# Score copies moved ahead of exponentials in five steps of a batch, and loads of rows and v placed in other steps

## The chip, the core and the metric

The kernel runs on one core of a Trainium2 chip. The core has five engines that run side by side, each with its own queue of instructions: TensorE (PE: matmuls, with its weight loads shown as PEld), VectorE (DVE), ScalarE (ACT), GpSimd (POOL) and SyncE (SP, which only issues transfers here). Matmul results land in a small memory called PSUM and have to be copied out of it by DVE or ACT. Transfers between DRAM and the on-chip memory are DMAs; they are issued by SP, ACT or POOL.

The metric is device time in microseconds, the median over runs of the whole kernel. Three runs of the kernel before took 2294.4, 2296.27 and 2301.48 us.

## The reference

Attention over 8 batches, 12 heads, 448 positions and 64 elements a head, with two small matrices that mix the heads, before and after the softmax; then a Fourier mixing over positions and channels with a two-layer network behind it.

```python
scores = scale * np.matmul(q, k.transpose(0, 1, 3, 2))
scores = np.einsum('bhij,hg->bgij', scores, w_pre)
attn = np.exp(scores - np.max(scores, axis=-1, keepdims=True))
attn = attn / (np.sum(attn, axis=-1, keepdims=True) + 1e-09)
attn = np.einsum('bhij,hg->bgij', attn, w_post)
x = np.matmul(attn, v)          # to (B, S, H * D)
...
u = x + np.real(np.fft.fft(np.fft.fft(x, axis=1), axis=2))
un = (u - mean(u)) / np.sqrt(var(u) + 1e-06)
out = u + np.maximum(un @ w_ch1, 0.0) @ w_ch2
```

All data is float32.

## The kernel before

The kernel has two phases. `mix_phase` does attention and the Fourier mixing and takes the first third of the time; `ffn_phase` does the network, with products of half and quarter blocks combined by sums (a Strassen scheme), so that its results are added up from several partial tiles.

**Attention in steps.** A batch is cut into 8 blocks of rows, and these into 23 steps (`GS`); 8 batches make 184 steps (`TOT`), numbered on through all batches. A main loop goes through the steps and emits the instructions of PE, DVE, ACT and POOL in an order that is kept as written (`manual_schedule`); each engine works its own queue in that order. In each step there are, for different positions of a pipeline:

- `pre` (L656): matmuls that mix the heads of the step two ahead, into two PSUM tiles `mx` of one buffer each. `max0` and `max1` (L663, DVE) take the row maxima, `exp0` and `exp1` (L670, ACT) the exponentials with their sums. A `mx` tile is free for the next step's `pre` when its exponential is done.
- `scale` (L677, L678 on DVE, L680 on POOL): the reciprocal of the sums, which needs both exponentials, and the scaling of the two halves.
- `post` (L690) and `turn` (L703, DVE): the second mixing of heads and its turning.
- `QK` (L628): the score matmuls of a block that comes eight steps later. Each call writes two of the four PSUM slots named `ms`, and leaves two copies from PSUM to `Sb` on ACT (L489). The copies are not emitted at once: they go into a list, `pend`.
- `AV` (L720), in 12 of 23 steps, and `full`: transposes of q and k (L601) and of results (L764), and the Fourier matmuls (L829, L845). All of them use `ms` slots, too.
- `gather` (L645): four DMAs on SP that bring the rows of one step out of `Sb` into `Kr`, five steps ahead. A block's `Sb` buffer is used again two blocks later; its first copy then waits for the last gather of the block before.
- `conv` (L250 to L310): one operation on DVE of a conversion of the network's weights.

`flush()` emits what stands in `pend`. It is called after `post`, before each `full` item, before a gather that needs a copy still pending, and at the end of odd steps. The orders of even and odd steps (by the global number, so that a batch step changes its parity from batch to batch) are:

```python
ORDERS = tuple(o.split() for o in (
    "pre post flush AV max0 exp0 "
    "QK max1 exp1 turn scale conv full gather",
    "pre post flush max0 max1 QK exp0 "
    "AV turn exp1 scale conv gather full flush"))
```

**Loads.** `due("none", at, fn)` puts a load at the beginning of step `at`. POOL issues most of them: rows of q and k of the next batch (`emit_load_qk`, two DMAs of 112 KB a call, two calls a tile, into four buffers `raw`), v (`emit_load_v`, one DMA of 224 KB a call), and in the last batch the first rows of the second phase (`lead.load`, into the same four buffers; their statistics are taken from step 5 of that batch on). For batch 0, q, k and v are loaded at step -40, ahead of everything; for batch 1 the first two row tiles follow at step -12. The six tiles of a batch's rows are transposed at steps 5, 9, 13, 15, 15 and 16 of the batch before.

**The end.** In `second2` the last tile's partial results are put on a timetable of numbered places (`on(place, ...)`), one for each matmul and some between. The very last tile has three output quarters, `v11`, `v12` and `v22`, that collect partial sums `j0` to `j6` on DVE (`vec`) or POOL (`pl`) with `both` (L1366) and `more` (L1357), and are stored by SP and ACT, one half each (`store`, L1373).

Of the kernel before, what the change touches and what calls it, by code (L numbers as in the profile page):

```python
# [45 lines left out]
GS = BLOCK_AT[-1]  # L46
# [42 lines left out]
AT_T = ((5, 9), (15, 16), (13, 15))  # L89
AT_L = ((-8, -7), (-6, -5), (-4, -3), (-2, -1), (8, 9), (10, 11))  # L90
AT_V = ((2, 3), (4, 4), (5, 6))
AT_L1 = ((-12, -12), (-12, -12), (2, 3), (4, 5), (8, 9), (10, 11))
AT_QK0 = {2: (-1, 0, 0), 3: (2, 3, 3), 4: (4, 5, 5)}
AT_QK = ((0, 2, 1), (0, 1, 2), (0, 1, 2), (1, 2, 2),
         (0, 1, 2), (0, 1, 2), (0, 1, 2), (0, 1, 2))
AT_AV = ((1, 2, 4), (0, 1, 3), (1, 3, 5), (1, 3, 4))
AT_X = ((13, 0), (23, 1), (28, 3), (29, 2))
AT_Z = (39, 40, 40, 42)
AT_S = ((42, 44), (46, 48))
# [351 lines left out]
def mix_phase(ctx, tc, rest, ident, q, k, v, w_pre, w_post, u_scr, u_rev, wts, lead):  # L451
# [39 lines left out]
    def flush():  # L491
        while pend:
            pend.pop(0)[1]()

    def room(n):
        if sum(e[0] for e in pend) + n > 4:
            flush()
# [79 lines left out]
    def emit_load_v(b, pr, y):  # L577
        if y == 0:
            batches[b]["v", pr] = pvv.tile([P, 2, C7 * D], F32, name="vv", tag=f"vv{pr}")
        h = 6 * y + 2 * pr  # L580
        nc.gpsimd.dma_start(
            out=batches[b]["v", pr][64 * y:64 * y + 64, :, :],
            in_=v[b, h:h + 2].rearrange("h (p c) d -> p h (c d)", c=C7))
# [301 lines left out]
    def due(kind, at, fn):  # L885
        fill[kind].append((at, len(fill[kind]), fn))
# [4 lines left out]
    for b in range(B):  # L891
        f = b * GS
        at_t = [(a, nm, xx) for xx, at in enumerate(AT_T) for nm, a in zip("qk", at)]
        if b == 0:

            for i, xx in enumerate(START):
                for j, nm in enumerate("kq"):
                    for y in range(2):
                        due("none", -40, lambda xx=xx, nm=nm, y=y: emit_load_qk(0, xx, nm, y))
                    due("full", 2 * i + j - 20, lambda xx=xx, nm=nm: emit_xpose(0, xx, nm))  # L900
                for n, at in enumerate((2 * i - 18, i - 13)):
                    due("QK", at, lambda n=n, xx=xx: (emit_qk(n, xx), n))
            for pr in range(3):
                for y in range(2):
                    due("none", -40, lambda pr=pr, y=y: emit_load_v(0, pr, y))
        else:
            for at, (a, nm, xx) in zip(AT_L if b > 1 else AT_L1, sorted(at_t, key=lambda e: e[0])):
                for y in range(2):
                    due("none", f + at[y] - GS if b > 1 else at[y],
                        lambda b=b, xx=xx, nm=nm, y=y: emit_load_qk(b, xx, nm, y))  # L910
            for xx, at in enumerate(AT_T):
                for nm, a in zip("qk", at):
                    due("full", f + a - GS,
                        lambda b=b, xx=xx, nm=nm: emit_xpose(b, xx, nm))
        for pr in range(3 if b else 0):
            for y in range(2):
                due("none", f + AT_V[pr][y], lambda b=b, pr=pr, y=y: emit_load_v(b, pr, y))
        for n in range(0 if b else 2, NBL):
            for xx in range(3):
                due("QK", AT_QK0[n][xx] if b == 0 and n in AT_QK0 else  # L920
                    f + BLOCK_AT[n] - 8 + AT_QK[n][xx],
                    lambda n=NBL * b + n, xx=xx: (emit_qk(n, xx), n))
        for n in range(NG):
            for pr in range(3):
                due("AV", f + GROUP_AT[n + 1] + AT_AV[n][pr],
                    lambda a=b * NG + n, pr=pr: (emit_av(a, pr), None))
            at, gi = AT_X[n]
            if b == B - 1 and n > 1:
                at += 2
            due("full", f + at, lambda g=groups[b * NG + gi]: emit_x(g))  # L930
        for n, at in enumerate(AT_Z):
            due("full", f + at, lambda b=b, n=n: emit_z(b, n // 2, n % 2))
        for pair in range(2):
            for par in range(2):
                due("full", f + AT_S[pair][par],
                    lambda b=b, pair=pair, par=par: emit_s2(b, pair, par))
    f = (B - 1) * GS
    due("none", f + 1, lambda: nc.gpsimd.memset(lead.mhalf[:, :], -0.5))
    for x in range(TB // P):
        for y in range(2):  # L940
            due("none", f - 4 + 2 * x + y, lambda x=x, y=y: lead.load(x, y))
        due("full", f + (5, 9, 11, 13)[x], lambda x=x: [lambda: lead.stats(x)])
        due("full", f + (15, 16, 19, 21)[x], lambda x=x: [lambda: lead.norm(x)])
        due("full", f + 18 + 2 * x, lambda x=x: lead.turn(x, ms_tile))
# [11 lines left out]
    def take(kind, s):  # L956
        large = 0
        while fill[kind] and fill[kind][0][0] <= s:
            fn = fill[kind].pop(0)[2]
            if kind == "none":  # L960
                large += bool(fn())
            elif kind == "full":
                flush()
                pend.extend((1, e, None) for e in fn())
            else:
                room(2)
                evs, n = fn()
                pend.extend((1, e, n) for e in evs)
        return large

    s = int(min(v_[0][0] for v_ in fill.values()))
    ET = mybir.EngineType
    with tc.manual_schedule(engines={ET.PE, ET.DVE, ET.Activation, ET.Pool}):
        while s <= TOT - GS + AT_X[-1][0]:
            old = len(later)
            n = take("none", s)
            ahead, now = 0 <= s + LM < TOT, 0 <= s < TOT
            for op in ORDERS[s % 2]:
                if op == "flush":
                    flush()  # L980
                elif op in fill:
                    take(op, s)
                elif op == "conv":
                    if s >= 4:
                        wts.deal(1)
                elif op == "gather":
                    if 0 <= s + LG < TOT:
                        if any(e[2] is not None and e[2] <= at_step[s + LG][0] for e in pend):
                            flush()
                        emit_gather(s + LG)  # L990
                elif op == "scale":
                    if ahead:
                        emit_scale(s + LM)
                    for _ in range(old if s < TOT + 5 else 0):
                        later.pop(0)()

                    if s < TOT - 3:
                        for _ in range(min(len(folds), 1 if n and s > 3 else 2)):
                            folds.pop(0)()
                elif op in ("post", "turn"):  # L1000
                    if now:
                        (emit_postmix if op == "post" else emit_turn)(s)
                elif ahead:
                    (emit_premix if op == "pre" else emit_max if op[0] == "m"
                     else emit_exp)(s + LM, *map(int, op[3:]))
            s += 1
        flush()
        wts.deal(1000)
# [42 lines left out]
def ffn_phase(ctx, tc, rest, ident, u_scr, u_rev, wts, ub_scr, out, fold_rest,  # L1051
# [262 lines left out]
    def second2(n, st):  # L1314
# [5 lines left out]
        vec = nc.vector  # L1320

        def on(s, fn, *a):
            at.setdefault(s, []).append(lambda: fn(*a))
# [52 lines left out]
        for j, i in enumerate(ORDER2):  # L1376
            b = 7 * j
# [13 lines left out]
        j0, j3, j5, j6, j4, j1, j2 = range(7)  # L1391
        v22, v12, v11 = range(7, 10)
        pl = nc.gpsimd
# [5 lines left out]
        if end:  # L1399
            for v, r, d in ((v11, 0, 0), (v12, 0, 1), (v22, 1, 1)):  # L1400
                on(0, load, v, r, d)
            on(27, out_, j3, 1, 0)
            on(41, both, vec, j6, j5)
            on(41, out_, j6, 1, 0)
            for s, *o in ((24, vec, v11, j0), (33, vec, j5, j0), (34, pl, v12, j5),
                          (41, pl, v22, j6), (44, vec, v12, j4), (51.5, vec, v11, j1),
                          (59, vec, v22, j4)):
                on(s, both, *o)
            on(52, store, v11, 0, 0)
            on(58, store, v12, 0, 1)  # L1410
            on(60, store, v22, 1, 1)
        else:
            for s, *o in ((33, j5, j0), (40, j6, j5), (47, j5, j4), (54, j0, j1),
                          (61, j5, j2), (62, j4, j6)):
                on(s, both, vec, *o)
            on(27, out_, j3, 1, 0)
            on(44, out_, j6, 1, 0)
            on(55, out_, j0, 0, 0)
            on(62, out_, j5, 0, 1)
            on(63, out_, j4, 1, 1)  # L1420
# [133 lines left out]
```

## Time and profile before

| What | us |
|---|---|
| median of three runs | 2296.27 |
| the profiled execution | 2299.42 |
| its span, first to last instruction | 2297.6 |
| PE busy | 2249.2 |
| DVE busy | 1711.2 |
| POOL busy | 1292.1 |
| ACT busy | 1167.1 |
| PE on the chain that ended last | 87% of the span |

The profile belongs to one execution. Its lines are read as follows. A line of the timeline has the start in us from the beginning of the span, the duration, the engine, the line of the kernel, the operation, the tiles it writes and reads (`out<-in`), their shapes, a count, and in brackets the idle time of the engine before it with what ended that. A line of the waits has who waited, for whom, the total in us, how often, and the longest. SP's and ACT's issuing of DMAs is marked SPq and ACTq.

Batches 1 to 6 of attention take 94 to 97.5 us each between their first premix matmuls, batch 0 takes 87.2; a step is 2.5 to 6.1 us long, most are 3.3 to 4.7.

### The profile page before, as it was taken

The numbers are of one execution on the slowest core, as the hardware profiler recorded it, in microseconds if no ns is written. First come the engines' busy times: TensorE is split into PE (matmuls) and PEld (weight loads), VectorE is DVE, ScalarE is ACT, GpSimd is POOL, SyncE is SP. The second block draws the span as 40 slices with busy tenths as digits, with TensorE's granted clock in tenths as the row PEclk, the third lists the DMA queues.
The fourth block names the chain that finished last, engine by engine and source line by source line (L and its number), as shares of the span: only waits on it lengthen the run. The fifth ranks groups of instructions, "written<-read, shape, count | busy, mean of one in ns | idle before, by whom it ended". The sixth has DMA issues, their size and how long they took to land.

```text
span 2297.6 us, 60793 instructions
## 1 busy us (share of the span) xinstructions
PE 2249.2 (98%) x22894; PEld 1740.7 (76%) x22894; DVE 1711.2 (74%) x3640; ACT 1167.1 (51%) x3330; POOL 1292.1 (56%) x1805
## 2 busy tenths in 40 slices
PE   7999999999999999999999999999999999999998
PEld 3455555555554677777899999999999899999998
DVE  5778787888877757776877787778778777765545
ACT  4676767767676533231445445444444445434434
POOL 7677878879768541221555555546555645454334
PEclk9999999999999999999999999999999999999999
DMA  7566565666756475649677887788787987795664
GB/s 185 168 178 181 168 192 171 190 179 181 202 151 190 143 265 182 230 162 327 191 181 180 252 214 184 212 195 242 204 197 184 277 188 174 191 257 121 143 146 76
DMA packets 228063, 439.45 MB, mean 191 GB/s; under 512 B 35964, under 2 KB 149558, under 8 KB 227772
## 3 DMA queue, kind: packets, MB, share of 16 engines
q1 hardware_dynamic: 156620, 301.52, 38.2%
q0 software_dynamic: 68864, 133.00, 30.4%
q8 instruction: 183, 3.00, 0.6%
q10 hardware_dynamic: 2288, 1.05, 0.2%
q14 instruction: 108, 0.88, 0.1%
HBM read 213.16 MB, written 143.16 MB: 155 GB/s over the span
## 4 chain that ended last, share of the span: by engine, by line
PE 87%; DVE 5%; DMA 3%; ACT 2%; issue 1%; POOL 1%; SPq 1%; ACTq 0%; DVEq 0%; POOLq 0%
PE psP L1213 18%; PE psP L1335 14%; PE psR L1213 9%; PE psR L1335 7%; PE mx L656 6%; PE ms L720 6%; PE ms L628 5%; PE po L690 5%; PE psQ L1213 4%; PE psQ L1335 3%; PE psP L1290 3%; PE ms L845 2%; PE ms L601 2%; DMA Kr<-Sb 1%; PE psR L1290 1%
## 5 line engine op out<-in xcount | busy, mean ns | idle before, releaser
L1369 POOL DMA_DIRECT2D out_dram<-od x172 | 209.1, 1276 | 261.7 <-DVE od L1357 175.3
L680 POOL TENSOR_SCALAR PP<-PP,rcp 128x448 f32<-128x448 f32 x368 | 234.6, 647 | 170.2 <-DVE rcp L678 123.8
L670 ACT ACTIVATE PP<-mx,nmx 128x448 f32<-128x448 f32 x368 | 230.2, 631 | 165.2 <-DVE nmx L663 157.2
L663 DVE TENSOR_REDUCE nmx<-mx 128x1 f32<-128x448 f32 x368 | 212.5, 618 | 101.2 <-PE mx L656 99.1
L1176 POOL TENSOR_TENSOR hq<-h 128x128 f32<-128x128 f32 (+1 forms) x210 | 130.0, 619 | 255.9 <-ACT h L1235 122.3
L1363 ACT COPY od<-psP 128x192 f32<-128x192 f32 x488 | 156.1, 320 | 172.0 <-PE psP L1335 170.6
L1366 DVE TENSOR_TENSOR od<-od 128x768 f32<-128x768 f32 x210 | 201.3, 972 | 52.7 <-ACT od L1363 52.3
L703 DVE STREAM_TRANSPOSE Pv<-po 128x896 f32<-128x896 f32 x184 | 203.7, 1107 | 2.9 <-PE po L690 2.1
L489 ACT COPY Sb<-ms 124x448 f32<-124x448 f32 (+1 forms) x378 | 181.7, 540 | 46.0 <-PE ms L628 19.2
L656 PE MATMUL mx<-Kr,kw 60*32 60x448 f32 x2944 | 192.2, 549 | 4.3 <-ACT PP L670 2.3
L628 PE MATMUL ms<-kT,qT 64*32 64x448 f32 (+1 forms) x3072 | 191.6, 545 | 3.9 <-ACT qT L489 2.8
L720 PEld LDWEIGHTS ms<-Pv,vv 64*64 64x64 f32 x5376 | 138.1, 132 | 73.7 <-issue 48.8
L690 PE MATMUL po<-PP,kw 60*32 60x448 f32 x2944 | 184.0, 537 | 1.2 <-POOL PP L680 1.1
L1213 PE MATMUL psP<-qs,w1t 128*128 128x256 f32 x744 | 179.2, 380 | 2.4 <-DVE h L1234 1.5
L1213 PE MATMUL psP<-ks,w1t 128*128 128x256 f32 x744 | 179.3, 380 | 0.4 <-DVE h L1234 0.3
L720 PE MATMUL ms<-Pv,vv 64*64 64x120 f32 (+1 forms) x5376 | 160.8, 263 | 3.6 <-ACT Sb L489 2.2
L254 POOL TENSOR_SCALAR wst<-wst 128x256 f32<-128x256 f32 (+1 forms) x76 | 118.6, 1569 | 67.2 <-ACT wst L265 66.9
L1213 PEld LDWEIGHTS psP<-qs,w1t 128*128 128x128 f32 x744 | 139.5, 190 | 19.4 <-DVE h L1234 1.9
L1213 PEld LDWEIGHTS psP<-ks,w1t 128*128 128x128 f32 x744 | 139.5, 190 | 17.2 <-DVE h L1234 0.7
L1213 PE MATMUL psP<-ub,w1t 128*128 128x256 f32 x528 | 127.2, 379 | 1.1 <-DVE h L1234 1.1
L1234 DVE TENSOR_TENSOR h<-h,psP 128x512 f32<-128x512 f32 x42 | 28.8, 686 | 127.9 <-PE psP L1213 112.3
L1335 PE MATMUL psP<-w2t,hq 128*128 128x192 f32 x490 | 122.5, 332 | 1.2 <-DVE od L1357 1.2
(199 smaller groups left out, 5301.6 us busy)
## 6 DMA issues: line engine op xcount, KB each, us to landing
Kr<-Sb SPq DMA_DIRECT2D x730, 105.0 KB
out_dram<-od POOLq DMA_DIRECT2D x172, 384.0 KB, 6.3
qs<-ub SPq DMA_DIRECT2D x89, 384.0 KB
ks<-ub SPq DMA_DIRECT2D x88, 384.0 KB
ub<-ub SPq DMA_DIRECT2D x79, 384.0 KB
w1t<-w SPq DMA_DIRECT2D x42, 384.0 KB
w2t<-w SPq DMA_DIRECT2D x42, 384.0 KB
raw<-in_moe_w_ch_dram SPq DMA_DIRECT2D x32, 384.0 KB
```

Source lines behind the costliest of these rows:

```text
L628: nc.tensor.matmul(pss[x][o:o + hi - lo, :S], st["qT", xx][64 * x:64 * x + 64, y, lo:hi], st["kT", xx][64 * x:64 * x + 64, y, :], start=Tr ...
L656: nc.tensor.matmul(mx[x][64 * z + o:64 * z + o + 32, :S], kw1[64 * x:64 * x + KR, o:o + 32], Kr[64 * x:64 * x + KR, z, :], start=True, sto ...
L663: nc.vector.tensor_reduce(nmx[:, :], steps[T]["mx"][x][:, :S], axis=AX.X, op=ALU.max, negate=True)
L670: nc.scalar.activation(steps[T]["PP"][:, x, :], steps[T]["mx"][x][:, :S], ACTF.Exp, bias=steps[T]["nmx", x][:, :], accum_out=steps[T]["den ...
L680: nc.gpsimd.tensor_scalar(PP[:, x, :], PP[:, x, :], rcp[:, x:x + 1], 1.0, op0=ALU.mult, op1=ALU.mult)
L690: nc.tensor.matmul(po[o:o + 32, z, :S], kw2[64 * z:64 * z + KR, y, :], PP[64 * z:64 * z + KR, :, c * HS:(c + 1) * HS], start=True, stop=True)
L703: nc.vector.transpose(turned[a]["Pv"][:, j, :].rearrange("p (z s) -> p z s", z=2), steps[T]["po"][:, :, :S])
L720: nc.tensor.matmul(pss[y][64 * x:64 * x + 64, :nu * R], st["v", pr][64 * y:64 * y + 64, x, jb * D:(jb + 1) * D], _ap(Pv, 64 * y * rp + 32 ...
L1213: mm = nc.tensor.matmul(p[:, m, :], w1[i][:, kc, m * P:(m + 1) * P], ub[:, kc, :], start=i in (0, 4, 1)[:3 - seed] and m == kc == 0, stop= ...
L1335: nc.tensor.matmul(ps[j, key][:, :DQ], a, b, start=m in (0, 4), stop=True, skip_group_check=True)
L1366: eng.tensor_tensor(D[j][:, :, :], D[j][:, :, :], D[k][:, :, :], op=ALU.add)
L1369: nc.gpsimd.dma_start(out=acc[t, r, d], in_=D[j][:, :, :], accum_op=ALU.add)
```

## The change

It makes four edits.

- A new list `TWO` names steps 0, 2, 5, 13 and 15 of a batch. In these, from step 0 on, `flush()` is called right after `QK`. In odd steps this places the copies of the scores on ACT before both exponentials, in even steps between the first and the second. Without it they come behind both.
- Batch 0's v is loaded at steps 0, 1, 3 and 4 instead of -40 (`AT_V0`), and all six row tiles of batch 1 get other steps (`AT_L1`): the first at -2 and -1, the others from 2 to 12.
- The first rows of the second phase are loaded four steps earlier, from step -8 relative to the last batch.
- In the last tile, the sum of `j6` into `v22` goes from POOL (place 41) to DVE (43), that of `j4` into `v22` from DVE (59, the last sum of all) to POOL (45), and `v22` is stored at place 57, ahead of `v12` at 58.

```diff
-AT_L1 = ((-12, -12), (-12, -12), (2, 3), (4, 5), (8, 9), (10, 11))
+AT_L1 = ((-2, -1), (2, 4), (5, 6), (7, 8), (9, 10), (11, 12))
+AT_V0 = ((0, 0), (1, 1), (3, 4))
...
+TWO = (0, 2, 5, 13, 15)
...
-            for pr in range(3):
-                for y in range(2):
-                    due("none", -40, lambda pr=pr, y=y: emit_load_v(0, pr, y))
...
-        for pr in range(3 if b else 0):
+        for pr in range(3):
             for y in range(2):
-                due("none", f + AT_V[pr][y], lambda b=b, pr=pr, y=y: emit_load_v(b, pr, y))
+                due("none", f + (AT_V if b else AT_V0)[pr][y], lambda b=b, pr=pr, y=y: emit_load_v(b, pr, y))
...
-            due("none", f - 4 + 2 * x + y, lambda x=x, y=y: lead.load(x, y))
+            due("none", f - 8 + 2 * x + y, lambda x=x, y=y: lead.load(x, y))
...
                 elif op in fill:
                     take(op, s)
+                    if op == "QK" and s >= 0 and s % GS in TWO:
+                        flush()
...
             for s, *o in ((24, vec, v11, j0), (33, vec, j5, j0), (34, pl, v12, j5),
-                          (41, pl, v22, j6), (44, vec, v12, j4), (51.5, vec, v11, j1),
-                          (59, vec, v22, j4)):
+                          (43, vec, v22, j6), (44, vec, v12, j4), (45, pl, v22, j4),
+                          (51.5, vec, v11, j1)):
                 on(s, both, *o)
             on(52, store, v11, 0, 0)
             on(58, store, v12, 0, 1)
-            on(60, store, v22, 1, 1)
+            on(57, store, v22, 1, 1)
```

## The prediction

> **What bounds the kernel now.** I read the page first: TensorE (PE) is busy 98% of the span and holds 87% of the chain that ended last, so only what makes PE wait, or what runs after its last matmul, can change the time.
>
> ```profile
> span 2297.6 us, 60793 instructions
> PE 2249.2 (98%) x22894; PEld 1740.7 (76%) x22894; DVE 1711.2 (74%) x3640; ACT 1167.1 (51%) x3330; POOL 1292.1 (56%) x1805
> ```
>
> The change lies in the attention part (to about 830 us) and in the last 12 us. So next the busy time by stretches of that part (columns: stretch, its length, then busy us and count of PE, PEld, DVE, ACT, POOL, the clock, the DMA share, GB/s), and PE's waits from 126 to 770 us (total, times, longest).
>
> ```profile
> 345.00:460.00 115.00, 113.01 (x2390) 61.41 (x2392) 91.92 (x200) 81.56 (x257) 94.55 (x150) 1.00 0.60 181
> ```
>
> ```profile
> PE ms L601 <- ACT Sb L489: 6.5, 17, 1.2
> PE ms L845 <- ACT Sb L489: 2.7, 6, 0.6
> PE ms L720 <- ACT Sb L489: 1.5, 1, 1.5
> PE po L690 <- POOL PP L680: 1.1, 4, 0.4
> ```
>
> The reader sees that PE runs almost gapless, that VectorE (DVE) is 80% busy beside it, and that the waits the copies' move aims at (a transpose or a second-FFT matmul waiting for a PSUM slot that holds scores) sum to 6.5 + 2.7 = 9.2 us, 0.4% of the span. Going through them by step, they sit in batch steps 2, 5, 13 and 15, all in the new list; step 0, also in it, shows none but a 1.1 us "issue" wait.
>
> Then one such step in the timeline, batch 4's step 5 and the step after (DVE, then ACT):
>
> ```profile
> 434.28 1.16 DVE L663 TENSOR_REDUCE nmx<-mx 128x1 f32<-128x448 f32 x2 [0.97 <-PE mx L656]
> 435.36 1.11 DVE L703 STREAM_TRANSPOSE Pv<-po 128x896 f32<-128x896 f32 x1
> 436.45 0.16 DVE L677 TENSOR_REDUCE rcp<-den 128x2 f32<-128x4 f32 x1
> 436.64 0.17 DVE L678 RECIPROCAL rcp<-rcp 128x2 f32<-128x2 f32 x1
> 436.72 1.29 DVE L310 TENSOR_TENSOR wst<-wst 128x256 f32<-128x256 f32 x1
> 437.94 1.12 DVE L489 COPY qT<-ms 128x512 f32<-128x512 f32 x1
> 438.89 1.11 DVE L663 TENSOR_REDUCE nmx<-mx 128x1 f32<-128x448 f32 x2
> ```
>
> ```profile
> 435.00 0.63 ACT L670 ACTIVATE PP<-mx,nmx 128x448 f32<-128x448 f32 x1 [0.46 <-DVE nmx L663]
> 435.63 0.62 ACT L670 ACTIVATE PP<-mx,nmx 128x448 f32<-128x448 f32 x1
> 436.24 0.96 ACT L489 COPY Sb<-ms 124x448 f32<-124x448 f32 x2
> ```
>
> DVE has no idle mark between 435.36 and the next step's max at 438.89: it goes on without a gap behind the reciprocal, and the reciprocal needs both exponentials.
>
> Last, ACT's wait in batch 7 and the tail:
>
> ```profile
> 729.68 0.97 ACT L489 COPY Sb<-ms 124x448 f32<-124x448 f32 x2 [3.66 <-DMA Kr<-Sb]
> ...
> 2291.72 1.73 SPq L1373 DMA_DIRECT2D out_dram<-od  x3
> ...
> 2292.14 0.95 DVE L1366 TENSOR_TENSOR od<-od 128x768 f32<-128x768 f32 x1
> ```
>
> **What the Trainium skill says.** "Perfetto Trace Analysis", section "Matmuls": independent matmul groups should rotate through PSUM banks so that one's evacuation overlaps the next one's matmuls. The trace agrees: the waits above occur just where the rotation over four `ms` slots comes back to a slot not yet copied. "DVE: scalar operands, raw-bit mode, write accounting and state across instructions", section 5: the DVE's queue is one in-order queue. So a late reciprocal holds all behind it; the seven DVE lines above run in program order. "DMA: Bandwidth & Descriptors", section "Issuing engines are not separate DMA queues": transfers from every issuing engine run on the same 16 engines and interleave. The trace agrees: with GpSimd's (POOL's) loads in flight, four of its six first gathers take 2.8, 3.7, 4.0 and 4.0 us to land.
>
> **Part 1, the copies in front.** In a listed step two (in doubled steps four) score copies of 0.41 us spacing go before both exponentials (odd global steps) or before the second (even ones). Worked for batch 4's step 5, an odd one, from t = 433.28 (first premix matmul). Scores start at 434.79; a copy can start 1.07 later (432.51 to 433.58 one step earlier): 435.86, second copy 436.27, exponentials 436.69 and 437.31, the last done with its accumulator read at 438.03. Gain: the transpose starts at 436.50, not 436.82 (0.32). Price: the reciprocal runs at 438.05, not 436.45 (+1.6), and behind it queue the weight operation (1.22 to the next start), the qT copy (0.95) and the next max, now 440.5. Its exponential ends at 441.9; the premix after next needs that PSUM slot and started at 440.99 before. So PE loses 0.9 to 1.1. With a short weight operation (0.27) the same sum ends at about even.
>
> The other listed steps, same method. Odd step 13: gain 0.3, next step longer (3.85, with AV), so the lateness is hidden: -0.1. Odd step 15: two DVE copies queue behind, and the next scores need the slot of the first: +0.5. Even steps 5, 13, 15: the reciprocal is only 1.0 late, -0.3 each where the weight operation is short. Step 2: 0.3 to 0.4 gained, given back through four 0.47 us DVE sums before the next max: +0.1 even, +0.4 odd. Step 0: no wait to gain; 0 even, +0.3 odd. Over batches 2, 4, 6 about +1.0 each; over 1, 3, 5 about 0; batch 7 +0.7: +3.7. All gains without prices: -9.2; prices at the long weight operations throughout: +7.5.
>
> Batch 0 has no slack yet on ACT: four copies at 39.70 to 41.53 follow the exponentials. In front of the second one (done 39.5), they push it to 41.4 and the reciprocal with it; the next exponential starts 1.1 later; step 2 repeats this with two copies (+1.0). The scores of step 3 and the gather at 49.77, which wait for them, come 2.1 later. SyncE then issues gathers back to back to 70, so nothing wins it back: +2.1 (0 if the gathers were not the limit). Steps 13 and 15 there: +0.4.
>
> **Part 2, the loads.** Taken from POOL's queue before 24 us: six v loads of 224 KB, eight row loads of 112 KB (all six row tiles of batch 1 get new steps). From 4 to 24 us the DMA share is above 1.0; the first premix waits to 28.08, 29.63 and 30.01 for gathers. At 2.6 us a gather (the shortest landing among the lead rows' loads) the last, issued at 26.58, is there at 29.2 instead of 30.0: -0.7 (bounds 0 and -1.2). They come back in steps -2 to 12. POOL's issues (0.6 and 0.72 each) lie beside its waits of 2 to 3 us for the reciprocal. Their 2.2 MB compete with gathers, one of which PE awaits for 1.0 us until 59.92: I take +0.3 (-0.5 to +1.5). The lead rows go four steps ahead, from about 682..715 to 665..698. The 16 DMA engines' share is 0.40 from 660 to 700 and 0.80 from 700 to 732, so they leave the full stretch for an empty one. The copy at 729.68 waits for a gather whose issue ended at 722.48, 7.1 us earlier, while POOL moved v, rows and weights; batch steps 6 and 7 there last 0.5 and 2.65 longer than in other batches. But batch 7 also lacks a transpose in step 5 (3.26 against 4.45), so its gathers have less time anyway: of 3.1 us I take -2.2 (0 to -3.1). The moved loads' buffers are free by then (transposes two steps ahead).
>
> **Part 3, the tail.** The 0.95 us sum at 2292.14 leaves DVE's end; one of 0.96 enters at 2286.4. Of it 0.67 fills a wait for ACT, the rest delays by 0.25 all that follows. SyncE issues three stores, the last at 2293.12. After: the first at 2291.97, v22's behind it 0.53 later, v12's next at 2293.0: -0.1 (bounds -0.6 and +0.5). POOL's sum takes the place of its former one (2288.35 to 2290.62) and is hidden.
>
> **Sum.** -0.7 + 0.3 - 2.2 + 2.1 + 0.4 + 3.7 - 0.1 = +3.5 us, against the profiled execution's 2299.42 (span 2297.6, 1.8 around it). That execution is 3.2 above the median 2296.27; on the median: 2299.8, stated as 2299.5.
>
> **The rivals.** Forecast, no change, 0.42: prices and gains cancel. A measurement of this kernel can tell about 0.3% (7 us) from no change, so from 2289.4 to 2303.2.
> Rival A, faster, 0.34: DVE's lateness is absorbed (it is idle 20%, and a weight operation shrinks when it slides off POOL's work), so all 9.2 us of slot waits go, with part of the half-hidden stretch before each (up to 3 more), and batch 7's 3.1 and the start's 0.7: -14, about 2283; the middle of this case is 2285. For it: max starts on PE's release in most steps. Against: the gapless DVE lines in step 5.
> Rival B, slower, 0.24: the reciprocal behind delayed exponentials becomes the bound. Place: DVE between reciprocal and next max in steps 0, 2, 5 and 15; price +7.5, with batch 0's +2.5 and crowded gathers +1.5, nothing won in batch 7: +11, about 2307. It decides once the wait of next max exceeds 1 us in a step followed by a short one.
> That the change doesn't do what it says: the copies could already be forced out by a gather; in listed steps the gather needs an older block, so no.
>
> Eight in ten: 2283 to 2309, from both rivals' ends; the forecast's own range is 2291 to 2303. Faster 0.34, same 0.42, slower 0.24.
>
> **What would show it.** Right: PE waits of L601 and L845 on ACT Sb nearly gone; the DVE reciprocal waiting 1.0 to 1.6 us for ACT PP in listed steps, odd ones more; premix waits on ACT PP growing by several us; the gather of step 3 issued near 52; batch 7's step 7 under 5 us; the last store within 0.5 of its place. Wrong: if batches 2, 4 and 6 shrink by over 1 us each, the DVE price was hidden and A holds; if they grow by over 2, B.

## The result, and the profile after

The changed kernel takes 2323.45 us (median of 6 runs, 2322.57 to 2327.86), the kernel before 2296.74 us beside it (6 runs): ratio 1.0113, 95% interval 1.0101 to 1.0125, or 26.7 us slower. The forecast was 2299.5, the range ended at 2309. In the changed kernel the code of the attention part stands two lines lower (L658 is the premix, before L656), the later part one line.

The page of the changed kernel, its first two lines:

```profile
span 2321.8 us, 60850 instructions
PE 2275.0 (98%) x22894; PEld 1759.0 (76%) x22894; DVE 1703.7 (73%) x3640; ACT 1167.0 (50%) x3330; POOL 1291.3 (56%) x1805
```

The span is 24.2 us longer and PE's busy time 25.8 us longer, with the same 22,894 matmuls. So nearly all of the loss is counted as work. The stretch shown of before, now:

```profile
345.00:460.00 115.00, 113.91 (x2261) 63.78 (x2261) 91.58 (x195) 79.36 (x247) 92.37 (x147) 1.00 0.60 178
```

PE is busy for 113.91 us instead of 113.01, and does 2261 matmuls instead of 2390. Part of that difference is that the stretch meets other steps now; the matmuls of this stretch took 111.9 us before (331.0 to 442.9). PE's waits from 126 to 800 us, which is nearly the same part of the work (total, times, longest):

```profile
PE mx L658 <- ACT PP L672: 5.2, 9, 1.9
PE ms L630 <- DVE kT L491: 3.4, 6, 0.7
PE ms L630 <- issue: 0.8, 1, 0.8
PE ms L603 <- ACT Sb L491: 0.5, 1, 0.5
```

The waits that the copies were moved for did go (6.5 + 2.7 us before, 0.5 now); the premix's wait for the exponentials and the score matmuls' wait for DVE's copies came in. All waits together are 10.1 us, against 15.6 before. The waits alone would call this kernel faster.

DVE's wait for the denominators from 126 to 770 us, before (L677) and after (L679):

```profile
DVE rcp L677 <- ACT PP L670: 7.3, 11, 2.8
```

```profile
DVE rcp L679 <- ACT PP L672: 59.5, 35, 3.4
```

It is in order that the loss is found. I take the time from the first premix matmul of each step to that of the next, in both traces. At batch 0's first step the change is 1.9 us ahead; then the batches are longer by 7.7, 5.6, 1.8, 1.5, 6.0, 2.8 and 2.6 us, batch 7 up to its last premix by 1.3: +27.4. Behind the attention part 3.2 us come back (1.1 before the first matmul of the next part, 1.9 near 1100 us, where the chain of before waits for transfers). By step, for batches 5 and 6, against the kernel before, in us (the steps left out differ by less than 0.1, but for step 11 of batch 6, where a gather wait of 0.7 went):

```
step              0     1     2     3     4     5     6     7    13    14    15    16    sum
change, b5     0.00 +0.26 +0.29 +0.66 +0.62 -0.61 +0.37 +0.59 -0.39 +0.12 -0.34 +1.21  +2.78
change, b6     0.00 +0.01 -0.06 +0.68 +0.22 -0.41 +0.71 +0.59 -0.25 +0.59 -0.21 +1.49  +3.36
e5 below, b5   0.00 +0.25 -0.22 +0.59  0.00 -0.76 +0.12 +0.35 -0.38 +0.12 -0.34 +0.12  -0.15
```

The listed steps 5, 13 and 15 themselves gain 0.2 to 0.6 here, near what was worked out (0.3). The steps behind them lose more. Single steps in which a score copy awaits a gather (step 13 of batch 4 is one) differ by 1 us and more between profiles of any of these kernels. So do whole batches: in e4 below, which leaves the attention part as it was, they differ from the kernel before by -0.8 to +1.9. A batch's difference of that size, taken from one profile, says little. Most of the loss in the table stands on firmer ground: steps 3, 6, 14 and 16 keep within 0.03 of the kernel before in batches 1 to 6 of e3, e4 and e7, which leave the order of these batches as it was. The other steps of the table don't.

**Where the time goes behind a listed step.** Two things can be seen. The first is on DVE. Batch 5, steps 15 and 16 (even order), DVE's timeline in the changed kernel (start, us, engine, line, operation):

```profile
592.86 1.11 DVE L705 STREAM_TRANSPOSE Pv<-po 128x896 f32<-128x896 f32 x1
595.10 0.16 DVE L679 TENSOR_REDUCE rcp<-den 128x2 f32<-128x4 f32 x1 [1.13 <-ACT PP L672]
595.29 0.17 DVE L680 RECIPROCAL rcp<-rcp 128x2 f32<-128x2 f32 x1
595.38 0.54 DVE L312 TENSOR_TENSOR wst<-wst 128x384 f32<-128x384 f32 x1
595.83 1.11 DVE L491 COPY qT<-ms 128x512 f32<-128x512 f32 x1
596.76 0.57 DVE L491 COPY kT<-ms 128x384 f32<-128x384 f32 x1
597.22 1.17 DVE L665 TENSOR_REDUCE nmx<-mx 128x1 f32<-128x448 f32 x2
```

and PE's, at the score matmuls of step 16, which need that kT:

```profile
597.48 0.98 PE L630 MATMUL ms<-kT,qT 64*32 64x448 f32 x16 [0.72 <-DVE kT L491]
```

The reciprocal stood 1.1 us idle for the second exponential; the two copies and the next max then stand behind it without a gap. The max starts 2.3 us after its step's premix (594.90); before the change it was 1.0 (premix at 572.66):

```profile
573.69 1.16 DVE L663 TENSOR_REDUCE nmx<-mx 128x1 f32<-128x448 f32 x2
```

This is the prediction's mechanism, in an even step for which it had counted a gain.

The second was not foreseen. PE's timeline in batch 4, step 14, the step behind an odd listed one, before:

```profile
469.26 0.98 PE L656 MATMUL mx<-Kr,kw 60*32 60x448 f32 x16
470.04 0.96 PE L690 MATMUL po<-PP,kw 60*32 60x448 f32 x16
```

and after:

```profile
487.77 1.20 PE L658 MATMUL mx<-Kr,kw 60*32 60x448 f32 x12
488.55 0.57 PE L692 MATMUL po<-PP,kw 60*32 60x448 f32 x4
488.79 0.56 PE L658 MATMUL mx<-Kr,kw 60*32 60x448 f32 x4
488.92 1.17 PE L692 MATMUL po<-PP,kw 60*32 60x448 f32 x12
```

The 16 premix matmuls belong to two halves of the array's rows, x = 0 and x = 1, and run side by side: 16 matmuls of 0.55 us each start within 0.45 us. (The Trainium skill, "TensorEngine Tiling (Array Packing)", section "Key Properties", says that different tiles can execute in parallel; the trace agrees.) Each half writes one PSUM tile, and there is one such tile for each half; it is free when its exponential has read it. Before the change both exponentials had long been done. Now the second one (487.60 to 488.2) ends after the premix has begun: eight matmuls of x = 0 run on their half alone, those of x = 1 come 0.6 later, and the post-mix is drawn out in turn. PE is never idle, and no wait is listed. The time from the first to the last premix matmul of a step, as far as it exceeds its usual 0.45 us, sums from batch 2 on to 1.4 us before and to 21.0 us after.

### The profile page after: what moved, and what is told of

Its sections match the earlier page's. It is cut to its first block, busy times and chain, and to the rows that moved or that the text cites. A ratio compares the mean times of both kernels' runs of the same rounds, so it can differ in the third digit from the quotient of the medians.

```text
span 2321.8 us, 60850 instructions
## 1 busy us (share of the span) xinstructions
PE 2275.0 (98%) x22894; PEld 1759.0 (76%) x22894; DVE 1703.7 (73%) x3640; ACT 1167.0 (50%) x3330; POOL 1291.3 (56%) x1805
## 5 line engine op out<-in xcount | busy, mean ns | idle before, releaser
L658 PE MATMUL mx<-Kr,kw 60*32 60x448 f32 x2944 | 218.3, 549 | 13.8 <-ACT PP L672 9.6
L630 PE MATMUL ms<-kT,qT 64*32 64x448 f32 (+1 forms) x3072 | 205.3, 544 | 7.9 <-DVE kT L491 3.9
L692 PE MATMUL po<-PP,kw 60*32 60x448 f32 x2944 | 207.8, 538 | 0.1
L630 PEld LDWEIGHTS ms<-kT,qT 64*32 64x32 f32 (+2 forms) x3072 | 64.5, 105 | 80.2 <-issue 54.6
```

The source lines that it names most:

```text
L630: nc.tensor.matmul(pss[x][o:o + hi - lo, :S], st["qT", xx][64 * x:64 * x + 64, y, lo:hi], st["kT", xx][64 * x:64 * x + 64, y, :], start=Tr ...
L658: nc.tensor.matmul(mx[x][64 * z + o:64 * z + o + 32, :S], kw1[64 * x:64 * x + KR, o:o + 32], Kr[64 * x:64 * x + KR, z, :], start=True, sto ...
L692: nc.tensor.matmul(po[o:o + 32, z, :S], kw2[64 * z:64 * z + KR, y, :], PP[64 * z:64 * z + KR, :, c * HS:(c + 1) * HS], start=True, stop=True)
```

## The experiments

e1 to e4 take the change apart.

**e1**, the copies in front alone:

```diff
+TWO = (0, 2, 5, 13, 15)
...
+                    if op == "QK" and s >= 0 and s % GS in TWO:
+                        flush()
```

> Only the scores' copies are put in front (TWO); loads and tail as before. Theory D (a late reciprocal holds DVE's queue, so the next max is late, in every batch): batches 2 to 6 grow as in the changed kernel (+1.8, +1.5, +6.0, +2.8, +2.6), batches 0 and 1 also carry most of their +7.7 and +5.6, and batch 7 loses 3.6: +28 to +33 us in all, ratio 1.012 to 1.014. Rival L (the loads moved into batches 0 and 1 cost those two batches most of their +13): +18 to +22 us, ratio 1.008 to 1.0095. The prediction's own sum for this part was +6.2 us (1.0027).

Measured: ratio 1.0117 (1.0102 to 1.0132), +27 us. Batches 2 to 6 grow by 1.9, 2.0, 6.8, 3.2 and 2.7, batches 0 and 1 by 8.4 and 5.9. The copies in front alone cost as much as the whole change. Theory D stands for the place; its mechanism is tried in e5.

**e2**, the loads of batch 0's v and batch 1's rows alone:

```diff
-AT_L1 = ((-12, -12), (-12, -12), (2, 3), (4, 5), (8, 9), (10, 11))
+AT_L1 = ((-2, -1), (2, 4), (5, 6), (7, 8), (9, 10), (11, 12))
+AT_V0 = ((0, 0), (1, 1), (3, 4))
```

> Only batch 0's v loads and batch 1's row loads get their new steps. Theory D: the start gains about 2 us (first premix near 25.2 instead of 28.1), batches 0 and 1 give little of it back: -2 to +1 us, ratio 0.999 to 1.0005. Rival L: the same start gain, then +8 to +11 us in batches 0 and 1: +6 to +9 us, ratio 1.003 to 1.004. The prediction's sum was -0.4 us.

Measured: 1.0028 (1.0015 to 1.0040), +6.4 us, as rival L said. The first premix comes at 25.2 us, but batch 0 is 9.3 us longer (steps 4, 5 and 7: +3.6, +1.3, +4.5). What those steps wait for, ACT's and PE's waits from 34 to 100 us:

```profile
ACT Sb L490 <- DMA Kr<-Sb: 9.2, 3, 6.0
```

```profile
PE mx L657 <- DMA Kr<-Sb: 4.3, 3, 1.5
```

Before, these were 2.9 and 0.2: the gathers land late.

**e3**, the lead rows alone (`f - 4` to `f - 8` in their loads' steps):

> Only the lead rows are loaded four steps earlier. Both theories: batch 7's step 7 falls from 6.7 to about 4.4 us and nothing else changes: -2.2 us (prediction -2.2, bounds 0 and -3.1), ratio 0.9990. If the stretch only moves the wait into another step of batch 7, 0.

Measured: 0.9995 (0.9984 to 1.0005), which can't be told from no change; batch 7's step 7 takes 4.98 instead of 6.71 us. But that step differs as much without the move: it takes 4.77 us in e1, which leaves the lead rows where they were, 5.68 to 8.48 in e2, e4, e6 and e7, which do so too, and 6.95 in e11, which moves them. In e11 the copy there still waits for its gather (3.66 us before):

```profile
729.61 0.97 ACT L489 COPY Sb<-ms 124x448 f32<-124x448 f32 x2 [3.87 <-DMA Kr<-Sb]
```

So the move's worth isn't shown.

**e4**, the tail alone (the last tile's sums and its store, as in the change's last part):

> Only the last tile's sums are dealt anew. Prediction -0.1 us (bounds -0.6 and +0.5); the changed kernel's last stretch (last matmul to span end) gives -0.4 with the last matmul 0.5 later. So -0.5 to +0.5 us, ratio 0.9998 to 1.0002.

Measured: 1.0004 (0.9995 to 1.0013): nothing.

**e6 and e7** divide e2: e6 moves the v loads alone (AT_V0), e7 the rows alone (AT_L1).

> Only batch 0's six v loads move from ahead of the start to steps 0 to 4. If the v loads are what steps 4, 5 and 7 of batch 0 wait behind in e2 (rival V: 1.3 MB issued between 37 and 50 us, just ahead of those gathers): start -1 us, batch 0 +5 to +9 us, total +4 to +8 us, ratio 1.002 to 1.0035. If it is the rows (rival R): about -1 us, ratio 0.9995.

> Only batch 1's row loads take their new steps. Rival R (the rows issued between 43 and 80 us crowd the gathers): batch 0 +5 to +9 us in steps 4 to 7, total +4 to +8 us, ratio 1.002 to 1.0035. Rival V: start -1 us and batch 0 within 1 us, total about -1 us. If it takes both together, each alone is under +2 us.

Measured: e6 1.0020 (1.0009 to 1.0030), +4.6 us; e7 0.9996 (0.9987 to 1.0006). It is the v loads. Each alone brings the first premix to 25.3 or 25.4 us, as both do: that gain comes once.

**e5**, the copies in front as in e1, with the reciprocal taken out of DVE's way:

```diff
                     if ahead:
-                        emit_scale(s + LM)
+                        held.append(s + LM)
+                        if not (s >= 0 and s % GS in TWO):
+                            release()
...
                 if op == "flush":
                     flush()
+                    if held and (held[0] < s + LM or i == len(ORDERS[1]) - 1):
+                        release()
```

> The copies in front as in e1, and in the listed steps the denominators' sum, the reciprocal and GpSimd's scaling are issued only behind the step's transposes' copies (just ahead of the next step's max), so that nothing of the next step stands in DVE's queue behind a late exponential. Theory D (the in-order DVE queue behind the reciprocal carries the price): steps 3, 4, 6, 7, 14 and 16 return to the lengths of the kernel before while the gains in steps 5, 13 and 15 stay; batches 2 to 6 fall to 95 us or below, the whole to -8 to +6 us against before (what stays is batch 0), ratio 0.9965 to 1.0026. Rival E (the exponentials themselves are late and hold the scores' slots and PSUM for the next premix, whatever stands behind them on DVE): still +18 to +27 us, ratio 1.008 to 1.012.

Measured: 1.0078 (1.0065 to 1.0091), +17.9 us: just below rival E's range, far from theory D's. DVE's wait for the exponentials at the reciprocal is back to what it was before the change (126 to 770 us):

```profile
DVE rcp L678 <- ACT PP L671: 6.6, 6, 3.0
```

With it went 9 us: step 16 falls from +1.2 and +1.5 to +0.12 (even order) and +0.59 (odd), step 4 to 0, step 7 in part. So the queue behind the reciprocal is at least a third of the price. At least, because e5 has a price of its own: with the reciprocal, GpSimd's scaling comes later too, behind other work in POOL's queue, and PE's post-mix waits for it (1.1 us in all before):

```profile
PE po L691 <- POOL PP L681: 4.6, 3, 2.8
```

The wait of 2.8 us is in batch 1's step 15, which is 3.9 us longer than before. With these 3.5 us given back, the queue's part would be nearer to a half; that is an estimate. What stays are the +0.5 to +0.6 behind the odd-order listed steps 5, 13 and 15 and most of batches 0 and 1. Batch 6's step 14 in e5, PE's timeline:

```profile
675.87 1.11 PE L657 MATMUL mx<-Kr,kw 60*32 60x448 f32 x12
676.65 0.56 PE L691 MATMUL po<-PP,kw 60*32 60x448 f32 x4
676.81 0.56 PE L657 MATMUL mx<-Kr,kw 60*32 60x448 f32 x4
677.02 1.09 PE L691 MATMUL po<-PP,kw 60*32 60x448 f32 x12
```

The same torn premix, with nothing late on DVE.

**e9** is e5 with other work put where the premix's second half is missing:

```diff
+            ops = list(ORDERS[s % 2])
+            if s > 0 and s % 2 == 0 and (s - 1) % GS in TWO:
+                ops[:2] = ops[1::-1]
```

> e5 with one thing more: in the even-order step that follows a listed odd one, the post-mix is issued ahead of the premix. Theory H (what e5 still pays is the premix's second half: it waits for the late second exponential, and until then PE works with one half of its rows, which is counted as busy): the post-mix fills that time, PE's busy time falls, the steps behind odd listed ones lose 0.3 to 0.6 us each (12 such steps in batches 2 to 7, the like in 0 and 1): -4 to -9 us against e5, +8 to +13 against before, ratio 1.0035 to 1.0055. Rival M (a step cannot be shorter than premix, max, exponentials in a row, so a later premix only makes the max and all behind it later): as e5 or slower, +15 to +22 us, ratio 1.0065 to 1.0095.

Measured: 1.0050 (1.0038 to 1.0062), +11.5 us: 6.4 less than e5, with intervals apart, as theory H said. From step 13's premix to step 17's, batch 0 is 0.72 longer than before in e5 and 0.26 shorter in e9; from step 0's to step 4's, batches 3, 5 and 7 are 0.4, 0.6 and 0.7 longer in e5 and 0.3, 0.1 and 0.3 shorter in e9. The whole 6.4 us isn't this alone: 2.4 are a stretch of half clock in batch 1 that e9 lacks (last section), and other steps differ either way. The same step of batch 6 in e9:

```profile
675.21 0.99 PE L691 MATMUL po<-PP,kw 60*32 60x448 f32 x16 [0.65 <-DVE Pv L704]
675.96 0.99 PE L657 MATMUL mx<-Kr,kw 60*32 60x448 f32 x16
```

The premix is whole again. The drawn-out premix time from batch 2 on is 21.2 us in e1, 14.6 in e5 and 9.6 in e9.

**e8**, e1 with the copies in front only in batches 0 and 1 (`0 <= s < 2 * GS`):

> The copies in front as in e1, but only in the listed steps of batches 0 and 1 (global steps below 46); loads and tail as before. If the two doubled batches carry half of the price because there four copies and a doubled group of score matmuls stand between the max and the exponentials (theory Q): batch 0 +8, batch 1 +6 as in e1, batches 2 to 7 as before: +12 to +15 us, ratio 1.005 to 1.0065. If the lateness of batches 0 and 1 is given back later by gathers that wait less (theory G): +5 to +9 us. The prediction's terms for these two batches gave +2.5 us.

Measured: 1.0050 (1.0035 to 1.0065), +11.5 us: just below what theory Q gave. Batch 0 is 4.5 and batch 1 5.9 us longer; the others differ by -0.5 to +1.0, as unchanged ones do. So batches 0 and 1 carry some 11 of e1's 27 us. Batch 1 shows how. Its step 2 has two calls of `QK`, and so four copies. ACT's timeline in its step 2, in the changed kernel:

```profile
141.53 1.84 ACT L491 COPY Sb<-ms 124x448 f32<-124x448 f32 x4 [1.29 <-PE ms L630]
143.22 0.67 ACT L672 ACTIVATE PP<-mx,nmx 128x448 f32<-128x448 f32 x1
143.84 0.66 ACT L672 ACTIVATE PP<-mx,nmx 128x448 f32<-128x448 f32 x1
```

and PE's:

```profile
144.04 1.20 PE L658 MATMUL mx<-Kr,kw 60*32 60x448 f32 x12 [1.85 <-ACT PP L672]
```

ACT stands 1.29 us for the score matmuls, does four copies, and only then the exponentials, though the max had long been there (139.97 to 141.1). The next premix, and PE with it, waits for them: +2.06 us. The step behind loses another 2.1 us, with no wait at all; see the last section. Batch 3's step 2 has the same four copies ahead of the exponentials and is only 0.2 longer: PE has eight Fourier matmuls (L847, 1.56 us) behind the scores there, and the step took 5.3 us before, batch 1's 3.0. So it needs a short step besides.

**e10** looks for the half of the idea that pays: the copies in front only in even-order steps 5, 13 and 15 of batches 1, 3 and 5, with the reciprocal behind, and the two harmless moves of loads:

```diff
+TWO = (5, 13, 15)
...
+                    if op == "QK" and GS <= s < 7 * GS and s % 2 == 0 and s % GS in TWO:
+                        flush()
```

> The copies in front only in listed steps 5, 13 and 15 with the even order, in batches 1, 3 and 5, with the reciprocal behind as in e5; and batch 1's row loads and the lead rows as in the change; v loads and tail as before. Theory H: each such step gains 0.3 to 0.7 and the step behind it gives back 0.12 only: -2.5 us, with batch 7's step 7 -1 to -2 and the rows 0 to -1: -3 to -6 us in all, ratio 0.9975 to 0.999. If the listed steps' gains are always given back behind them, as in the odd order: -2 to +1 us, ratio 0.999 to 1.0005.

Measured: 1.0010 (0.9996 to 1.0024), no gain. Step 5 does gain (-0.38, -0.61, -0.76, though step 4 ahead of it is 0.2 and 0.3 longer in batches 3 and 5, as in e4) and step 6 gives back 0.12, but step 7 of the same batches is 0.3, 0.8 and 1.0 longer. In batches 3 and 5 PE's post-mix waits 0.56 and 0.74 us there for the scaling of step 5, which stands behind GpSimd's next loads, as in e5; the 0.3 of batch 1 comes with no wait, and e4 has 0.4 there without any such change. PE's wait for the scaling from 126 to 770 us, and the longest one, in batch 1's step 15:

```profile
PE po L691 <- POOL PP L681: 4.8, 6, 2.9
```

```profile
186.26 1.04 PE L691 MATMUL po<-PP,kw 60*32 60x448 f32 x16 [2.92 <-POOL PP L681]
```

Half clock follows (last section), and that step is 4.1 us longer than before. So e10 doesn't show that the even-order half of the idea can't pay: holding the reciprocal back takes more than the copies give.

**e11** has only batch 1's rows and the lead rows moved (e7's and e3's edits):

> The two moves of loads that cost nothing alone (batch 1's rows, lead rows) together, without the v loads, without the copies in front, tail as before. If their small gains add (0.9996 and 0.9995 alone): -2 us, ratio 0.9991; a version faster than both kernels by what can be told (0.3%) would need -7 us and is not expected. If the rows crowd batch 0's gathers once more, 0 to +3 us.

Measured: 0.9988 (0.9979 to 0.9997), 2.8 us faster than before, less than the 0.3% asked for above. It has the lowest ratio of all these kernels, but its interval overlaps those of e3 and e7.

**e12** is the change with the v loads left ahead of the start (AT_V0 all at -40):

> The whole change, but batch 0's v loads back ahead of the start. Alone the v loads cost +4.6 us (e6). Theory S (that cost lies beside the lateness that the copies in front make in batch 0, and so is not paid twice): -2 to +2 us against the changed kernel, +24 to +29 against before, ratio 1.0105 to 1.0125. Rival (it is paid in full in the change too): -4 to -6 us against the changed kernel, ratio 1.0085 to 1.0095.

Measured: 1.0114 (1.0099 to 1.0128) against 1.0113 for the change. What the v loads cost alone is not paid beside the copies. That batch 0 is late already is the likely reason; it wasn't tried apart.

## Why the prediction was wrong

Point by point, by the terms of its sum:

- Start, -0.7: batch 0's first step is 1.9 earlier. Mis-sized: the gathers' landings didn't become shorter (GpSimd's first ones 3.6 to 4.9 us, against 2.8 to 4.0), but the first one is issued 2.8 us earlier (22.5 against 25.4). One pair of profiles is rough here: that step comes at 34.0 to 35.2 us in the seven kernels with moved start loads and at 35.2 to 37.0 in the other seven, 1.5 apart in the mean.
- Loads in batches 0 and 1, +0.3 (up to +1.5): alone +6.4, with the start's gain in it (e2), of it +4.6 by the v loads (e6). Mis-sized by far; in the change it is covered (e12), so it didn't spoil the sum.
- Lead rows, -2.2: step 7 of batch 7 went from 6.71 (the longest step before) to 4.37, -2.3. The number came true; that the lead rows did it isn't shown. With the copies in front and the rows unmoved the step takes 4.77 (e1), with the rows moved and no copies in front in that batch 4.98, 5.89 and 6.95 (e3, e10, e11).
- Tail, -0.1: from the last stage's matmuls to the end +0.1. Right, and too small to tell (e4).
- Batch 0's copies, +2.1 and +0.4: e8 shows +4.5, e1 +8.4 (the same code there; e1's trace has a stretch of half clock in batch 0, e8's has none). The gather of step 3 was issued at 51.82, "near 52" as forecast, but from a start 1.9 to 2.9 us earlier; by its own count it was some 4 to 5 late and not 2.1.
- Batches 1 to 7, +3.7 ("about +1.0 each" for 2, 4, 6, "about 0" for 1, 3, 5): the step that failed. The measured sum of 2 to 6 alone is 14.7, and batch 1 has 5.6; e1 and e12 have 16.5 and 14.9, and 5.9 and 5.6. The gains in the listed steps were right (0.3 said, 0.2 to 0.6 found). Two prices were missing. For one, "-0.3 each" for the even steps 5, 13 and 15 took DVE's slack as given: behind step 15 two copies and the max queue, and step 16 of batches 2 to 6 lost 1.2 to 1.5, where +0.5 (odd) and nothing (even) were said (e5 gives most of this back). For the other, the exponential was followed to "the premix after next", not to the very next one. The numbers were there: the second exponential of step 5 was to end at about 437.9 (437.31 and 0.62) and the next premix to begin at 437.4 (437.73 before, less the 0.32 gained), in the same PSUM tile.
- What made that second price invisible was the first sentence: "only what makes PE wait, or what runs after its last matmul, can change the time". 98% busy was read as 98% used. A half-filled array counts as busy (the same 22,894 matmuls, 25.8 us more), so this price showed in no wait that the gain of 9.2 us could be weighed against.

The signs named for it: L601's and L845's waits nearly gone, reciprocal waits in the listed steps, the premix's waits on PP up, step 7 of batch 7 under 5 us, all came; the last one shows little, as e1 has it without the moved rows. Batches 4 and 6 grew by over 2 us, 2 by 1.8: rival B's sign. B was right in direction and on DVE's part; its +11 us had no place for the torn premix, and too little for batches 0 and 1.

What stays open: e9 still pays 11 us, some 8 of it in batches 0 and 1, and its trace has 4.4 us of waits for GpSimd's scaling; no run has the copies in front with neither the queue behind the reciprocal nor a later scaling. How the 27 us divide between the two prices is therefore known only roughly. That four copies before the exponentials are what costs batch 1 its 4 us is read from the timeline, not tried by moving two of the four.

## What to carry to other kernels

Before work is put in front of an instruction that frees a buffer, set the new end of that instruction against the next writer of the same buffer, half by half where the buffer comes in halves; following the queue behind it isn't enough. Where matmuls share the array by rows, read PE's busy time together with the matmuls done in it: a lost partner shows as busy time, not as a wait. And take a move that covers several sites apart by site: here the listed steps gained what they were meant to, and the steps behind most of them gave back more. When an instruction is moved back, what another engine makes of its result moves too: the later reciprocal of e5 and e10 put GpSimd's scaling behind other work. And before a shorter step is put down to a move, look at the same step in kernels without the move.

## What the runs showed of the hardware

After a stretch in which PE had too little to do, it runs at half clock for a while. The windows of the changed kernel around the stall in batch 1 (142.18 to 144.04; the granted clock is the third value from the right):

```profile
141.94:145.36 3.42, 1.57 (x32) 0.58 (x28) 0.83 (x5) 2.66 (x8) 0.15 (x1) 1.00 0.34 99
145.36:148.77 3.41, 3.41 (x50) 1.83 (x40) 2.46 (x6) 1.34 (x4) 3.15 (x5) 0.50 0.35 129
148.77:152.19 3.42, 3.42 (x90) 1.67 (x88) 1.25 (x3) 1.69 (x7) 3.38 (x7) 1.00 0.64 189
```

The clock falls to 0.50 about 1.3 us after the stall has ended and is back 3.4 us later; post-mix matmuls take 0.95 us instead of 0.54, and the step is 2.1 us longer. In e9, where the post-mix stands in that stall and no wait over 0.9 us is left there, the clock stays at 1.00, and steps 2 and 3 together last 8.98 us instead of 11.33. In the v loads' kernel e6 it is the stall for a late gather:

```profile
52.62:56.03 3.41, 1.22 (x13) 0.17 (x5) 1.49 (x4) 0.65 (x2) 1.90 (x4) 1.00 0.68 164
56.03:59.44 3.41, 3.41 (x36) 1.70 (x44) 1.25 (x2) 1.91 (x5) 1.35 (x2) 0.50 0.89 206
```

Between 34 and 800 us the 14 traces have 17 such stretches. Each is 3.41 us long, and within a trace they begin whole multiples of 3.41 us apart. Cut into windows along these multiples, the traces give 3125 windows. All 11 windows in which PE was busy for less than 48% were followed by half clock, of 23 with 48 to 63% 6 were, and of the others none. So the stall's length alone doesn't decide. A stall of 2.48 us in e8 (739.79 to 742.27) lies across two windows, in which PE is still busy for 75% and 52%, and the clock stays:

```profile
737.22:740.64 3.42, 2.57 (x42) 1.19 (x38) 2.17 (x6) 0.18 (x2) 3.36 (x8) 1.00 0.79 180
740.64:744.05 3.41, 1.76 (x53) 1.53 (x56) 0.62 (x1) 2.36 (x7) 1.55 (x3) 1.00 0.73 212
744.05:747.46 3.41, 3.41 (x78) 1.19 (x70) 1.68 (x5) 2.64 (x11) 2.16 (x3) 1.00 0.51 170
```

The kernel before has no such stretch there. The Trainium skill, "TensorE: Matmul & The Clock Gate", section "Part 1: The HAM clock gate", gives the half clock, but after an idle window of about 3.4 us; the length fits, but here the measurement decides, and PE need not be idle in all of it: a stall of 1.85 us was enough. So in batch 1 this stall cost about 4. In e2's batch 0 there are two such stretches: by this estimate up to 4 of its 9.3 us are the clock, not the transfers.
